# A third group's second layer as seven block products, with the weight sums moved earlier

## The chip, the cores and the metric

The kernel runs on one core of a Trainium2 chip. The metric is the device time of one execution in microseconds (us). The engines are TensorE (PE; PEld is its weight load), VectorE (DVE), ScalarE (ACT), GpSimd (POOL) and SyncE (SP, which issues most transfers here). Each engine works through its own queue in order and waits on semaphores for the others.

## The reference

Two stages follow each other. The first is a linear attention with decay over 4 batches, 8 heads, 768 positions and head size 64, in blocks of 64 positions; the second takes its output as x (4 x 768 rows of 512) through a layer norm and two dense layers.

```python
intra = einsum('bhic,bhjc->bhij', qb, kb) * Dmask          # lam ** (i - j), lower triangle
out   = einsum('bhij,bhjd->bhid', intra, vb) + einsum('bhid,bhde->bhie', qb * lam_pow, kv_state)
kv_state = lam ** block * kv_state + einsum('bhsd,bhse->bhde', kb * rev_pow, vb)
...
xn  = (x - mean) / sqrt(var + 1e-6) * g_ln
out = x + maximum(xn @ w_ch1, 0) @ w_ch2                   # w_ch1 512 x 2048, w_ch2 2048 x 512
```

## The kernel before

The 3072 rows are cut into 12 windows of 256 positions of one batch (`NU = 12`), called pairs below: a pair holds two tiles of 128 rows. Pair u belongs to batch u mod 4, so four pairs in a row are independent and pair u + 4 needs the state that pair u left. The attention's part of pair u yields x, its mean and `xc` = (x - mean) * g. The two dense layers work on groups; group g is pair g.

**The attention's part of a pair.** `in_k_one`, `in_q_one` and `in_v` cast and scale the loaded k, q, v (L231, L236, L242) on the engine that the call names. `transpose_kq(u, a, eng)` transposes k (a = 0) or q (a = 1) on TensorE into a PSUM bank of the tag `sc` (L260) and copies it to SBUF on `eng` (L261). `kv` makes the key-value products (L321), `scores` the block scores (L276) into two banks of the tag `mm` ("sce", early) or `sc`, `mask` multiplies them by the triangle on VectorE (L286), `new_state` sums and decays the state (L331 on VectorE, L327 on GpSimd), `av` and `inter` add up the output (L433, L446), `norm` takes x, its mean and `xc` (L472, L473 on ScalarE, L474 on VectorE), `rstd_of` takes the squares and the root on ScalarE (L514, L515) and the reciprocal on VectorE (L519), and `to_xT` transposes `xc` (L504) and copies it on ScalarE (L505). `s12` is kv, both scores and the masks of a pair; `Y(u)` interleaves kv and scores of pair u with the output of pair u - 1; `X(u)` does so for the later pairs, whose blocks are cut differently (`kv64`, L386; `scores64`, L367; `mask64`, L373).

**The dense layers.** Layer 1 of a group (`m1`) is eight units of eight 128x256 matmuls (L541), each with a relu on ScalarE into `hT` (L544). For some quarters of some groups `m1.tile` cuts the unit by tile instead: 16 matmuls of 128x128 (L652), relu L655. The dict `tiles` says which.

Layer 2 has two forms. The plain one (`m2`) makes for each of two tiles 16 matmuls of 128x512 (L681) in four parts; a part named in `M2_SPLIT` is made as eight matmuls of 128x256. A finished tile is scaled and added to x by one VectorE instruction (L705). The block form (`m2.w`) treats hidden rows in pairs and output columns in halves as 2x2 blocks and makes seven block products instead of eight, 56 matmuls of 128x256 (L576), in four PSUM banks a to d: P1 into a, P2 into b, P7 into c, P5 into d, and then P6, P4 and P3 added on top of a, c and d. Each product is evicted when it is done: P1 and P7 by ScalarE and an add on GpSimd (L600 and L601, L608 and L609), the others by VectorE (L589). The block form needs sums of blocks of `hT`, made per group by `h_sums` on VectorE (L559, L560, L561, in two halves, 0 to 4 and 4 to 8), and sums of blocks of W2, made once by `w_sums(c, n)` for each quarter c (L806 and L807 for n = 0, L809 and L810 for n = 1, 16 instructions in all). Groups from `WG` on use the block form. The tiles `hs13`, `hs2`, `hs4` have one buffer each.

**What sets the order.** The order is written out by hand: `plan` is the list of dense units (eight of layer 1 and eight of layer 2 per group), and `units(n)` takes the next n; the calls between stand where each engine's queue is to have them. PSUM has four banks of the tag `mm`, used in turn by layer 1, layer 2, kv and the early scores: who comes next must wait until the instruction that reads the bank four uses ago is done. Two banks carry the tag `sc`, in turn too.

Of the kernel before, what the change touches and what calls it, by code (L numbers as in the profile page):

```python
# [17 lines left out]
def kernel(  # L18
# [11 lines left out]
    nc = tc.nc  # L30
# [9 lines left out]
    KB = DF // 128  # L40
# [1 line left out]
    NWC = 4  # L42
    eps = 1e-6
    XS = 64.0
    WG = 3
    M2_SPLIT = [(t, i) for t in (3, 5) for i in range(4)] + [(1, 3), (2, 3)]
    assert D == 64 and S % W == 0 and DM == 512

    ctx.enter_context(tc.manual_schedule())
# [43 lines left out]
    def load_in(u, name, eng):  # L93
        got = qkv_in[u][name]
        fill(got, name, u, slice(0, H), eng)
        qkv_in[u][name] = got.rearrange("p h (j d) -> p h j d", j=2)
# [132 lines left out]
    def in_k_one(u, eng, j):  # L229
        src = qkv_in[u]["k"].rearrange("p (a e) j d -> p a e j d", e=2)  # L230
        (eng.copy if eng is nc.scalar else eng.tensor_copy)(part(0, st[u]["kq"], ALL)[:, :, :, j], src[:, :, :, j])  # L231

    def in_q_one(u, eng, j):
        src = qkv_in[u]["q"].rearrange("p (a e) j d -> p a e j d", e=2)
        lq = (lam_q[:, :, j] if u < LB else lam_p[:, 0, :]).rearrange("p (a e) -> p a e", e=2)
        eng.tensor_tensor(part(1, st[u]["kq"], ALL)[:, :, :, j], src[:, :, :, j],  # L236
                          lq[:, :, :, None].to_broadcast([128, NP, 2, D]), op=ALU.mult)

    def in_v(u, eng, hs=ALL):
        n = hs.stop - hs.start  # L240
        lv = lam_v[:, hs, :, None] if u < LB else lam_p[:, 1, hs, None, None]
        eng.tensor_tensor(st[u]["vb"][:, hs], qkv_in[u]["v"][:, hs], lv.to_broadcast([128, n, 2, D]), op=ALU.mult)  # L242
# [248 lines left out]
    def to_xT(u, ab):  # L491
        s = st[u]
        t = 2 * u + ab
        g = group_of[t]
        i = t - groups[g][0]
        if i == 0:
            xT_of[g] = gp.tile([128, KA, GT * 128], BF16, tag="xT", bufs=3, name="xT")
        dst = xT_of[g][:, :, i * 128:(i + 1) * 128]
        if u < 2:
            xt = mm_tile([128, KA, 128], BF16, "xt")  # L500
        else:
            xt = ps.tile([128, KA, 128], BF16, tag=f"po{ab}", name="xt")
        for kk in range(KA):
            nc.tensor.transpose(xt[:, kk, :], s["xc"][:, ab, kk * 128:(kk + 1) * 128], ident)  # L504
        nc.scalar.copy(dst, xt)  # L505

    def rstd_of(u):
        s = st[u]
        std = wk.tile([128, 2], F32, tag="std", name="std")
        if "sum" in s:  # L510
            ss = xp.tile([128, 2], F32, tag="ss", name="ss")
            for ab in range(2):
                sq = wk.tile([128, DM], BF16, tag="sq", bufs=1, name="sq")
                nc.scalar.activation(sq, s["x"][:, ab], ACT.Square, bias=s["nmean"][:, ab:ab + 1], accum_out=ss[:, ab:ab + 1])  # L514
            nc.scalar.activation(std, ss, ACT.Sqrt, bias=eps_t, scale=XS * XS / DM)  # L515
        else:
            nc.scalar.activation(std, s["mv"][:, :, 1], ACT.Sqrt, bias=eps_t, scale=XS * XS)
        rstd = xp.tile([128, 2], F32, tag="rstd", name="rstd")
        nc.vector.reciprocal(rstd, std)  # L519
        x_keep[u] = (s["x"], rstd)  # L520
# [5 lines left out]
    def mlp(g):  # L526
# [134 lines left out]
        def m2(i, part):  # L661
            t = groups[g][i]
            if t == 2 * NU - 1:
                w = DM // 2
                if part % 2 == 0:
                    acc[i] = mm_tile([128, w], F32, "pm2h")
                z = part // 2
                for kk in range(part % 2 * 8, part % 2 * 8 + 8):
                    nc.tensor.matmul(acc[i], lhsT=hT[:, kk, i * 128:(i + 1) * 128],
                                     rhs=w2[kk // W2K][:, kk % W2K, z * w:(z + 1) * w],  # L670
                                     start=(kk == 0), stop=(kk == KB - 1))
                if part % 2 == 1:
                    finish_half(t, acc.pop(i), z, w)
                return
            if part == 0:
                acc[i] = mm_tile([128, DM], F32, "pm2")
            n_z = 2 if (t, part) in M2_SPLIT else 1
            for kk in range(part * 4, part * 4 + 4):
                for z in range(n_z):
                    zs = slice(z * DM // n_z, (z + 1) * DM // n_z)  # L680
                    nc.tensor.matmul(acc[i][:, zs], lhsT=hT[:, kk, i * 128:(i + 1) * 128], rhs=w2[kk // W2K][:, kk % W2K, zs],  # L681
                                     start=(kk == 0 and z == 0), stop=(kk == KB - 1), skip_group_check=t in (1, 2, 3, 5))
            if part == KB // 4 - 1:
                finish(t, acc.pop(i))

# [114 lines left out]
    def w_sums(c, n):  # L800
        v = w2[c].rearrange("p (k e) d -> p k e d", e=2)
        w = DM // 2
        b11, b12, b21, b22 = v[:, :, 0, 0:w], v[:, :, 0, w:], v[:, :, 1, 0:w], v[:, :, 1, w:]
        t1, t2, t3, t4 = (wt[c][:, :, i] for i in range(4))
        if n == 0:
            nc.vector.tensor_tensor(t1, b12, b11, op=ALU.subtract)  # L806
            nc.vector.tensor_tensor(t3, b12, b22, op=ALU.add)  # L807
        else:
            nc.vector.tensor_tensor(t2, b11, t3, op=ALU.subtract)  # L809
            nc.vector.tensor_tensor(t4, t2, b21, op=ALU.add)  # L810
# [86 lines left out]
    def s3(u):  # L897
        av(u, range(NP))
        inter(u, 0)
        if st[u]["S"][0][1] is None:  # L900
            norm(u, 0)
# [34 lines left out]
    def Y(u, sums=None):  # L936
        kv(u)
        av(u - 1, range(NP))
        inter(u - 1, 0, fence=False)
        reader(u - 1, act=True)  # L940
        scores(u, 0)
        scores(u, 1, early=True)
        inter(u - 1, 1)
        new_state(u, 0, nc.gpsimd)
        if sums is None:
            mask(u, 0, (0,))
        else:
            mask(u, 1, (0,))
        new_state(u, 1, nc.gpsimd)
        if sums is not None:  # L950
            mask(u, 1, (1,))
            m2s[sums].sums(4, 8)
        norm(u - 1, 0)
        norm(u - 1, 1)
        if sums is None:
            mask(u, 1)
            mask(u, 0, (1,))
# [91 lines left out]
    plan += [(m2b, 1, part) for part in range(KB // 4)]  # L1049
    for g in range(2, len(groups)):  # L1050
        m1, m2 = mlp(g)
        tiles = {2: (0, 1, 2), 5: (3,), 6: (2, 3), 7: (1, 2)}.get(g, ())
        for c in range(NWC):
            plan += [(m1.tile, c, i) for i in range(2)] if c in tiles else [(m1, 2 * c + i) for i in range(2)]
        if g >= WG:
            plan += [(m2.w, n) for n in range(8)]
        else:
            plan += [(m2, i, part) for i in range(len(groups[g])) for part in range(KB // 4)]
# [3 lines left out]
    def units(n):  # L1062
        for _ in range(n):
            f, *a = next(steps)
            f(*a)
# [18 lines left out]
    nc.scalar.activation(sqrt_first, eps_t, ACT.Sqrt)  # L1084
    rstd_of(0)
    rstd_of(1)
    units(2)
    open_window(3)
    in_k_one(3, nc.gpsimd, 0)
# [2 lines left out]
    in_v(3, nc.gpsimd)  # L1092
    units(2)
    s3(2)
    units(2)
    s4(2)
    in_k_one(3, nc.vector, 1)
    load_in(4, "v", nc.sync)
    units(2)
    to_xT(2, 0)  # L1100
    units(1)
    rstd_of(2)
# [10 lines left out]
    load_in(5, "v", nc.sync)  # L1113
    units(1)
    in_v(4, nc.gpsimd)
    units(3)
    w_sums(0, 0)
    transpose_kq(3, 0, nc.scalar)
    units(1)
    transpose_kq(3, 1, nc.scalar)  # L1120
    units(1)
    w_sums(0, 1)
    w_sums(1, 0)
    units(3)
    s12(3)
    units(5)
    w_sums(1, 1)
    open_in(6, False)
    load_in(6, "k", nc.sync)
    w_sums(2, 0)  # L1130
    w_sums(2, 1)
    w_sums(3, 0)
    units(1)
    transpose_kq(4, 0, nc.scalar)
    load_in(6, "q", nc.sync)
    units(1)
    transpose_kq(4, 1, nc.scalar)
    units(1)
    Y(4)
    open_window(5)  # L1140
    in_k_one(5, nc.gpsimd, 0)
    in_k_one(5, nc.gpsimd, 1)
    in_q_one(5, nc.gpsimd, 0)
    in_q_one(5, nc.gpsimd, 1)
    in_v(5, nc.gpsimd)
    load_in(6, "v", nc.sync)
    units(2)
    rstd_of(3)
    units(1)
    to_xT(3, 0)  # L1150
    to_xT(3, 1)
    open_in(7, False)
    units(1)
    w_sums(3, 1)
    open_window(6)
    transpose_kq(5, 0, nc.scalar)
    in_k_one(6, nc.gpsimd, 0)
    in_k_one(6, nc.gpsimd, 1)
    units(1)
    transpose_kq(5, 1, nc.vector)  # L1160
    units(1)
    in_q_one(6, nc.vector, 1)
    in_q_one(6, nc.vector, 0)
    store(0)
    units(2)
    m2s[3].sums(0, 4)
    units(4)
    load_in(7, "k", nc.sync)
    load_in(7, "q", nc.sync)
    load_in(7, "v", nc.sync)  # L1170
    open_window(7)
    Y(5, sums=3)
    open_in(8, False)
    units(4)
    in_v(6, nc.gpsimd)
    units(2)
# [14 lines left out]
    rstd_of(4)  # L1191
    in_k_one(7, nc.vector, 1)
    in_v(7, nc.gpsimd)
    units(2)
    X(6, rest=False)
    in_k_one(7, nc.scalar, 0)
    open_window(8)
    store(1)
    store(2)
    mask64(6, 1)  # L1200
    m2s[4].sums(0, 4)
    units(4)
    m2s[4].sums(4, 8)
# [192 lines left out]
```

## Time and profile before

| | |
|---|---|
| median of 3 runs | 219.79 us (218.43, 219.79, 221.13) |
| profiled execution | 220.35 us, span 218.6 us |
| TensorE clock granted | 1.00 |
| busy: PE, PEld, DVE, ACT, POOL | 206.5, 177.5, 141.8, 144.4, 86.2 us |
| W2 transfers landed (quarters 0 to 3) | 36.71, 39.34, 42.25, 45.30 us |
| group 2: layer 1, layer 2 on TensorE | from 55.30 to 63.3, from 63.33 to 73.4 us, with other work between |
| pair 3's scores, pair 4's Y | from 59.24, from 67.77 us |
| group 3's first layer-1 unit | from 73.84 us |

The profiled execution lasts 1.75 us longer than its span, which runs from the first to the last instruction. Times in the profile count from the span's start. A matmul's own duration in the trace contains the time in which it passes through; how many are made in a time is read from start to start. Idle time of an engine that is not the bound costs nothing by itself; what counts is what TensorE waits for.

### The profile page before, as it was taken

How to read it: one execution, taken by the hardware profiler on the slowest of the kernel's cores; microseconds unless marked ns; L12 is line 12 of the kernel's file. 1: busy time of each engine (PE TensorE's matmuls, PEld its weight loads, DVE VectorE, ACT ScalarE, POOL GpSimd, SP SyncE). 2: the span in 40 equal slices, each digit the busy share in tenths (PEclk: the TensorE clock that was granted, in tenths of full speed). 3: DMA queues.
4: the chain of work that ended last, by engine and by line, in shares of the span. 5: the costliest groups of instructions: out<-in, count | busy, mean ns of one | idle time of the engine just before them, and what ended most of it. 6: DMA issues, size and time to landing. Idle time of an engine off the chain costs nothing.

```text
span 218.6 us, 8079 instructions
## 1 busy us (share of the span) xinstructions
PE 206.5 (94%) x3525; PEld 177.5 (81%) x3525; DVE 141.8 (65%) x286; ACT 144.4 (66%) x315; POOL 86.2 (39%) x120
## 2 busy tenths in 40 slices
PE   1897999999999999999999989999999999999992
PEld 0586788559977988889889889999889889889881
DVE  2688351535896968868596764578775765866243
ACT  2788478444747765597876795876896875854630
POOL 5656058119712915922761280453291212002020
PEclk9999999999999999999999999999999999999999
DMA  3999999999999899958699021030030020220303
GB/s 107 300 244 182 164 270 192 202 305 269 298 204 224 200 215 260 232 111 165 127 237 241 13 48 51 3 99 3 3 96 3 20 79 3 57 45 3 96 0 96
DMA packets 64421, 29.88 MB, mean 137 GB/s; under 512 B 38529, under 2 KB 61569, under 8 KB 64386
## 3 DMA queue, kind: packets, MB, share of 16 engines
q1 hardware_dynamic: 59776, 24.97, 47.2%
q0 software_dynamic: 4224, 4.19, 12.2%
q8 instruction: 27, 0.44, 0.9%
q10 hardware_dynamic: 386, 0.20, 0.4%
q14 instruction: 8, 0.07, 0.1%
HBM read 27.27 MB, written 6.29 MB: 153 GB/s over the span
## 4 chain that ended last, share of the span: by engine, by line
PE 78%; ACT 7%; DMA 6%; DVE 5%; issue 1%; POOL 1%; POOLq 0%; DVEq 0%
PE pm L541 27%; PE pm L681 10%; PE pm1t L652 8%; PE pwa L576 6%; PE pwc L576 6%; PE pwd L576 5%; DMA w<-in_moe_w_ch_dram 4%; PE tp L260 3%; PE pwb L576 3%; DVE x L589 2%; DMA lam_b<-in_lam_dram 2%; PE xt L504 2%; ACT hT L544 1%; PE po L446 1%; ACT sq L514 1%; PE po L433 1%
## 5 line engine op out<-in xcount | busy, mean ns | idle before, releaser
L541 PE MATMUL pm<-xT,w 128*128 128x256 bf16 x608 | 70.9, 273 | 2.2 <-DMA w<-in_moe_w_ch_dram 1.5
L541 PEld LDWEIGHTS <-w 128*128 128x128 bf16 x608 | 58.2, 98 | 9.6 <-DMA w<-in_moe_w_ch_dram 1.7
L544 ACT ACTIVATE hT<-pm 128x512 f16<-128x512 f32 x76 | 44.3, 597 | 19.8 <-PE pm L541 19.6
L576 PEld LDWEIGHTS <-hs 128*128 128x128 f16 x288 | 27.2, 98 | 2.9
L601 POOL TENSOR_TENSOR x<-ev_u,x 128x256 f32<-128x256 f32 x9 | 6.6, 730 | 55.3 <-ACT ev_u L600 43.5
L327 POOL TENSOR_TENSOR Sn<-Stmp,lam_s 128x256 bf16<-128x256 f32 x16 | 9.9, 622 | 41.7 <-DVE Stmp L405 22.8
L559 DVE TENSOR_TENSOR hs<-hT 128x1024 f16<-128x1024 f16 x18 | 15.4, 856 | 15.0 <-ACT hT L544 12.7
L261 ACT COPY kqT<-tp 128x1024 bf16<-128x1024 bf16 x16 | 16.2, 1012 | 12.4 <-PE tp L260 12.4
L681 PE MATMUL pm<-w,hT 128*128 128x256 f16 (+1 forms) x136 | 22.7, 317 | 0.0
L576 PEld LDWEIGHTS <-hT 128*128 128x128 f16 x216 | 20.7, 98 | 2.3
L652 PE MATMUL pm1t<-xT,w 128*128 128x128 bf16 x320 | 19.3, 219 | 0.4 <-ACT xT L505 0.3
L652 PEld LDWEIGHTS <-w 128*128 128x128 bf16 x320 | 18.4, 98 | 1.0 <-issue 0.7
L681 PEld LDWEIGHTS <-hT 128*128 128x128 f16 x136 | 12.7, 98 | 6.0
L505 ACT COPY xT<-xt 128x512 bf16<-128x512 bf16 x24 | 14.0, 589 | 4.7 <-PE xt L504 4.2
L472 ACT ACTIVATE x<-po 128x512 f32<-128x512 f32 x18 | 10.6, 590 | 8.7 <-PE po L446 5.3
L655 ACT ACTIVATE hT<-pm1t 128x512 f16<-128x512 f32 x20 | 11.8, 597 | 5.6 <-PE pm1t L652 5.5
L474 DVE SCALAR_TENSOR_TENSOR xc<-po,nmean,g_row 128x512 bf16<-128x512 f32 x18 | 12.8, 743 | 2.1 <-ACT nmean L473 2.1
L514 ACT ACTIVATE sq<-x,nmean 128x512 bf16<-128x512 f32 x18 | 13.0, 721 | 0.3
L589 DVE SCALAR_TENSOR_TENSOR x<-pwd,rstd,x 128x256 f32<-128x256 f32 x18 | 8.6, 480 | 5.5 <-POOL x L609 5.3
L242 POOL TENSOR_TENSOR vb<-vin,lam_v 128x1024 bf16<-128x1024 f32 (+1 forms) x7 | 11.8, 1688 | 0.1
L242 POOL TENSOR_TENSOR vb<-vin,lam_p 128x1024 bf16<-128x1024 f32 x6 | 11.4, 1898 | 0.0
L589 DVE SCALAR_TENSOR_TENSOR x<-pwa,rstd,x 128x512 f32<-128x512 f32 (+1 forms) x18 | 10.3, 611 | 1.3 <-PE pwa L576 0.7
(141 smaller groups left out, 382.3 us busy)
## 6 DMA issues: line engine op xcount, KB each, us to landing
out_dram<-x SPq DMA_DIRECT2D x22, 256.0 KB, 3.8
w<-in_moe_w_ch_dram POOLq DMA_DIRECT2D x8, 512.0 KB, 8.5
kin<-in_k_dram SPq DMA_DIRECT2D x14, 256.0 KB, 5.0
qin<-in_q_dram SPq DMA_DIRECT2D x14, 256.0 KB, 5.4
vin<-in_v_dram SPq DMA_DIRECT2D x14, 256.0 KB, 5.2
kin<-in_k_dram SPq DMA_DIRECT2D x5, 512.0 KB, 6.7
qin<-in_q_dram SPq DMA_DIRECT2D x5, 512.0 KB, 6.9
vin<-in_v_dram SPq DMA_DIRECT2D x5, 512.0 KB, 7.3
```

Source lines behind the costliest of these rows:

```text
L242: eng.tensor_tensor(st[u]["vb"][:, hs], qkv_in[u]["v"][:, hs], lv.to_broadcast([128, n, 2, D]), op=ALU.mult)
L261: (eng.copy if eng is nc.scalar else eng.tensor_copy)(s["kqT"][:, a], tp)
L474: nc.vector.scalar_tensor_tensor(xc, in0=po, scalar=nm, in1=g_row, op0=ALU.add, op1=ALU.mult)
L505: nc.scalar.copy(dst, xt)
L514: nc.scalar.activation(sq, s["x"][:, ab], ACT.Square, bias=s["nmean"][:, ab:ab + 1], accum_out=ss[:, ab:ab + 1])
L541: nc.tensor.matmul(pm[:, b, :], lhsT=w1[n // W2K][:, kk, (n % W2K) * 128:(n % W2K + 1) * 128], rhs=xT_of[g][:, kk, 0:N], start=(b == 0 and ...
L544: nc.scalar.activation(hT[:, u * NB:(u + 1) * NB, 0:N], pm, ACT.Relu)
L559: nc.vector.tensor_tensor(s13, b[:, :, 1:2, :].to_broadcast([128, n, 2, 128]), b[:, :, 0:4:3, :], op=ALU.subtract)
L576: nc.tensor.matmul(pr[bank], lhsT=lhs(r), rhs=rhs, start=(first and r == 0), stop=(r == KB // 2 - 1), skip_group_check=True)
L589: nc.vector.scalar_tensor_tensor(out, in0=in0, scalar=r[ab], in1=in1, op0=ALU.mult, op1=ALU.add)
L652: nc.tensor.matmul(pm[:, b, :], lhsT=w1[c][:, kk, b * 128:(b + 1) * 128], rhs=xT_of[g][:, kk, i * 128:(i + 1) * 128], start=(b == 0 and kk ...
L681: nc.tensor.matmul(acc[i][:, zs], lhsT=hT[:, kk, i * 128:(i + 1) * 128], rhs=w2[kk // W2K][:, kk % W2K, zs], start=(kk == 0 and z == 0), s ...
```

## The change

`WG` goes from 3 to 2: group 2 (the third) uses the block form, so its layer 2 is 56 matmuls of 128x256 instead of 16 of 128x512 and 32 of 128x256. Its three uses of `m1.tile` become two, and the one of group 5 goes. `M2_SPLIT` names other parts of the first two groups' layer 2. All `w_sums` calls move forward, to lie between `rstd_of(1)` and `s12(3)`. `Y(4)` gets group 2's second half of `h_sums`, its masks of the first head pair move behind `to_xT(3, ...)`, and it stands behind all of group 2's layer 1 instead of inside its layer 2; the q copy of pair 4 moves to VectorE. Pair 5's q and v products on GpSimd stand behind group 2's first products. `Y(5)` stands one layer-1 unit earlier, and the second half of group 3's `h_sums` follows that unit instead of standing inside `Y`. `X(6)` stands one unit earlier.

```diff
-    WG = 3
-    M2_SPLIT = [(t, i) for t in (3, 5) for i in range(4)] + [(1, 3), (2, 3)]
+    WG = 2
+    M2_SPLIT = [(3, i) for i in range(4)] + [(t, i) for t in (0, 1, 2) for i in (2, 3)] + [(t, 1) for t in (1, 2)]
...
         if sums is not None:
             mask(u, 1, (1,))
-            m2s[sums].sums(4, 8)
+            if sums < 3:
+                m2s[sums].sums(4, 8)
...
-        tiles = {2: (0, 1, 2), 5: (3,), 6: (2, 3), 7: (1, 2)}.get(g, ())
+        tiles = {2: (0, 1), 6: (2, 3), 7: (1, 2)}.get(g, ())
...
     rstd_of(1)
+    w_sums(0, 0)
     units(2)
...
     s3(2)
+    w_sums(0, 1)
     units(2)
     s4(2)
     in_k_one(3, nc.vector, 1)
+    w_sums(1, 0)
     load_in(4, "v", nc.sync)
     units(2)
+    w_sums(1, 1)
     to_xT(2, 0)
...
     in_v(4, nc.gpsimd)
+    w_sums(2, 0)
     units(3)
-    w_sums(0, 0)
+    w_sums(2, 1)
     transpose_kq(3, 0, nc.scalar)
     units(1)
     transpose_kq(3, 1, nc.scalar)
     units(1)
-    w_sums(0, 1)
-    w_sums(1, 0)
+    w_sums(3, 0)
+    w_sums(3, 1)
     units(3)
     s12(3)
-    units(5)
-    w_sums(1, 1)
+    units(3)
+    m2s[2].sums(0, 4)
     open_in(6, False)
     load_in(6, "k", nc.sync)
-    w_sums(2, 0)
-    w_sums(2, 1)
-    w_sums(3, 0)
-    units(1)
     transpose_kq(4, 0, nc.scalar)
+    transpose_kq(4, 1, nc.vector)
+    units(1)
     load_in(6, "q", nc.sync)
-    units(1)
-    transpose_kq(4, 1, nc.scalar)
-    units(1)
-    Y(4)
+    Y(4, sums=2)
     open_window(5)
     in_k_one(5, nc.gpsimd, 0)
     in_k_one(5, nc.gpsimd, 1)
+    units(4)
     in_q_one(5, nc.gpsimd, 0)
     in_q_one(5, nc.gpsimd, 1)
     in_v(5, nc.gpsimd)
     load_in(6, "v", nc.sync)
-    units(2)
     rstd_of(3)
-    units(1)
+    units(2)
     to_xT(3, 0)
+    mask(4, 0, (0,))
+    units(1)
     to_xT(3, 1)
+    mask(4, 0, (1,))
     open_in(7, False)
     units(1)
-    w_sums(3, 1)
     open_window(6)
+    units(1)
     transpose_kq(5, 0, nc.scalar)
...
     transpose_kq(5, 1, nc.vector)
-    units(1)
     in_q_one(6, nc.vector, 1)
     in_q_one(6, nc.vector, 0)
...
     m2s[3].sums(0, 4)
-    units(4)
+    units(3)
...
     Y(5, sums=3)
     open_in(8, False)
+    units(1)
+    m2s[3].sums(4, 8)
     units(4)
...
     in_v(7, nc.gpsimd)
-    units(2)
+    units(1)
     X(6, rest=False)
...
     mask64(6, 1)
+    units(1)
     m2s[4].sums(0, 4)
```

## The prediction

> **What bounds the kernel.** I read the page's busy shares first, then busy time by stretch around the edits, then the chain that ended last, then the engines' timelines from 40 to 106 us.
>
> ```profile
> PE 206.5 (94%) x3525; PEld 177.5 (81%) x3525; DVE 141.8 (65%) x286; ACT 144.4 (66%) x315; POOL 86.2 (39%) x120
> ```
>
> TensorE is the bound; VectorE has a third of the span free, but that is an average. By stretch (length, then PE, PEld, DVE, ACT and POOL busy with counts, granted clock, DMA share, GB/s):
>
> ```profile
> 40.00:56.00 16.00, 16.00 (x201) 10.86 (x200) 8.30 (x19) 6.79 (x19) 8.08 (x9) 1.00 1.10 269
> 56.00:76.00 20.00, 20.00 (x415) 16.97 (x413) 17.65 (x30) 13.24 (x27) 9.66 (x11) 1.00 1.01 228
> 76.00:92.00 16.00, 16.00 (x296) 14.11 (x295) 13.24 (x25) 9.08 (x21) 8.71 (x10) 1.00 1.00 235
> 92.00:100.00 8.00, 7.91 (x221) 7.02 (x220) 5.22 (x12) 7.47 (x21) 3.03 (x5) 1.00 0.49 103
> ```
>
> TensorE never stops from 40 to 92 us, at full clock. Each saved PE microsecond counts, and so does each new PE wait. VectorE is 88% busy (17.65 of 20) where group 2 works. The chain names the one place nearby where another engine sets the pace, X(6):
>
> ```profile
> 94.70 0.29 ACT std L515
> 95.00 0.97 ACT hT L544 x2
> 96.08 0.38 PE po L446 x16
> ```
>
> TensorE's second `inter` of pair 5 waits there for ScalarE's queue, 0.09 us (8.00 less 7.91). Last, VectorE's timeline (start, length):
>
> ```profile
> 55.72 1.13 DVE L809 TENSOR_TENSOR wt<-w,wt 128x512 f16<-128x512 f16 x1
> 56.88 2.01 DVE L810 TENSOR_TENSOR wt<-wt,w 128x512 f16<-128x512 f16 x1
> ...
> 62.74 0.41 DVE L809 TENSOR_TENSOR wt<-w,wt 128x512 f16<-128x512 f16 x1
> ```
>
> The same W2 sum takes 0.41 us when GpSimd idles and 2.01 beside GpSimd's `vb` (56.52 to 58.61): it ends 0.28 after `vb` does. Instructions with a PSUM input, as L705, keep their 0.75 us there. So a sum waits out the GpSimd instruction in progress, and the next GpSimd instruction waits for the sum.
>
> **TensorE's work.** Group 2's layer 2 now is one plain tile and one split tile. Four 512-wide matmuls run from 48.08 to 48.94 (0.215 each), eight 256-wide from 53.98 to 54.85 (0.109): 16 x 0.215 + 32 x 0.109 = 6.93 us. Seven products are 56 x 0.109 = 6.10. Two layer-1 quarters (group 2's third, group 5's last) leave 128-wide halves (64 in 3.57 us, so 1.79 per quarter) for 256-wide ones (16 x 0.109 = 1.75): -0.04 each. Six more layer-2 parts of groups 0 and 1 are split, each 8 x 0.109 - 4 x 0.215 = +0.01. Together **-0.85 us**.
>
> **Added on the others.** VectorE gets six half-sums of group 2 (row means 0.86, 0.43, 0.45, twice: 3.5 us) and six evictions of 0.47 to 0.75 (3.1 us) for two L705 (1.5). ScalarE gets two evictions of 0.48, GpSimd two adds of 0.74. The sixteen W2 sums only move. The built order of instructions shows 56 L576 matmuls in place of group 2's 48 L681, so the change does what it says. SP's transfers keep their order; pair 5's k landed at 57.8 and is first used at 70.8, so no transfer turns late.
>
> **W2 sums ahead of the masks.** Chunk 0's four fit VectorE's idle times at 42.0 to 44.1 and 45.7 to 47.2, where it waits for TensorE and ScalarE: free, and 0.4 us late for each sum if that cover were gone, since the `xc` behind them feeds transposes at 47.85 and 48.94. Their data landed (by 45.3 for the last chunk). Chunks 1, 2 and 3 stand from 48.2 on ahead of pair 3's masks, with four L705 between, and beside an unbroken GpSimd row: two q products (1.01 each start to start), `vb` (1.87), two casts (0.58), two q, `vb`: 8.9 us. I alternate the queues as the rows do. Chunk 1 ends at 51.5 (L705 of 49.14 then goes 2.2 us late, but its PSUM bank is wanted only at 55.3), chunk 2 at 56.7, the fourth L705 at 57.4 (bank wanted at 57.98: 0.6 to spare), chunk 3 at 60.9. Pair 3's first mask starts at **60.8 instead of 59.68**. TensorE has three units (2.6 us) behind the scores, until 62.4, and then transposes pair 4's k into the bank of the third mask, now done at 63.0; the fourth is done at 63.6. Waits 0.58 + 0.15 = **+0.7**. Ends: 0 if the masks start by 60.3, 2.0 if sums and GpSimd run wholly one after the other (masks at 62.1).
>
> [...]
>
> **Pair 4's q copy.** `transpose_kq(4, 1)` goes from ScalarE to VectorE, behind mask, state sum (0.4) and group 2's first three half-sums (1.5, about 0.5 more if the state decay on GpSimd comes between). It ends at 66.5; Y(4), begun at 64.9, reaches the scores 0.9 later, at 65.8. **+0.5** (ends 0.25 and 0.7). In the products, pwb's bank waits for the second state sum: +0.1 (ends 0 and 0.1).
>
> **P3 of group 2.** rstd_of(3) now stands on ScalarE behind `ev_p`, and its reciprocal on VectorE ahead of P5's eviction, whose bank P3 continues. From P7's end: `ev_p` 0.6, two squares and the root 2.0 (93.00 to 95.00 in X(6)), reciprocal and eviction 0.5: 3.1. TensorE needs 3 x 0.87 + 0.22 = 2.8: 0.3 late; with POOL's adds behind two casts, and the second `xc` ahead of pwb's eviction, 0.6. I take **+0.45**, and 0.1 for the xT copy behind the squares (ends 0 and 0.6 together).
>
> **Group 3.** The last layer-1 unit moves behind Y(5). Its relu then stands behind norm's ScalarE work, which ended 3.76 us after Y's start (85.13 less 81.37); relu till 4.36, TensorE asks at 4.32; the second half-sum ends near 5.2, asked at 5.0. **+0.2** (ends 0 and 0.5). Pair 5's q and v products on GpSimd wait behind group 2's adds, till 74.7 and 76.6; TensorE asks for q at 76.9, for v at 81.7: nothing, but one for one if GpSimd ran over 2.2 us later.
>
> **X(6) a unit earlier.** The chain above is ScalarE's: one relu less (0.49) ahead of the fence, against 0.87 of TensorE's: 0.09 + 0.87 - 0.49 = 0.47 instead of 0.09, **+0.4** (ends 0 and 0.45).
>
> **Sum.** -0.85 + 0.7 + 0.5 + 0.1 + 0.55 + 0.2 + 0.4 = +1.6. The profiled execution took 220.35 (span 218.6 and 1.75 around it): 221.95. It lies 0.56 over the median of the three runs, 219.79, which gives 221.4; I say **221.7**. All low ends: 0.25 of waits, -0.6; all high: 2.0 + 0.7 + 0.1 + 0.6 + 0.5 + 0.45 = 4.35, +3.5.
>
> **Rivals.** *The saving arrives (0.27).* If GpSimd's row leaves gaps, the masks start by 60.3, the later waits overlap (a TensorE held at the scores gives the P3 chain time), and the net is -0.85 to +0.2: 219.5 from the profiled run, 218.9 from the median. For it: TensorE has no wait in 40 to 92 today, VectorE idles 7.7 us in 40 to 56, and the W2 sums that filled 74.3 to 76.9 are gone. Against: GpSimd's row from 48.8 to 58.6 is unbroken, and P3's wait follows from queue order alone.
>
> *VectorE becomes the bound (0.08).* VectorE's own work from 48.2 until pair 4's last mask near 76 is about 22 of 28 us (sums 5.0, L705 2.8, eight masks 4.9, state work and the q copy 2.0, half-sums 3.1, `xc` 1.4, evictions 2.7, small ones 0.5); the 18 instructions with two SBUF inputs each may wait for a GpSimd instruction. Past 60.3, each microsecond of mask delay is one of TensorE's. It decides if the first mask starts after 64: then 3.7 of transposes' wait and the other 1.75, less 0.85, +4.6: 225.0 or 224.4, slower than before by over 2%.
>
> *The other moves gain something that I miss (0.05).* TensorE idles 0.6 us in 125 to 130 and 0.26 in 105 to 125; if the new order closed all, and no wait came: 220.35 - 0.85 - 0.9 = 218.6.
>
> **Numbers.** Forecast 0.60, its own range 220.4 to 223.3. Over 80% with the saving and the high ends: 218.7 to 223.9. A difference of 2% (4.4 us) is about what a measurement of this kernel can tell from no change. Faster by that: 0.02, the product form is worth 0.4%. Slower: the VectorE case, 0.08. Within: 0.90.
>
> **What will show it.** Pair 3's first L286 mask at 60 to 61.5; an idle time of TensorE before the L260 transposes near 63, ended by VectorE; one before Y(4)'s L276, ended by L261 on VectorE; one before the last pwd of group 2, ended by L589 behind a reciprocal; 0.3 to 0.5 us before L446 in X(6), ended by ScalarE; busy TensorE down by 0.85. I am wrong if TensorE stays unbroken through 60 to 76, or if a transfer or a bank that I called spare ends a wait.

## The result, and the profile after

The changed kernel took **221.92 us** (median of 10 runs, 220.5 to 224.78), the kernel before 219.28 us beside it (10 runs, 218.43 to 221.13). The ratio is **1.0105** (95% interval 1.0068 to 1.0142): 1.5 to 3.1 us slower, which is less than the 2% named above and more than nothing. The profiled execution took 221.99 us, span 220.3. The ratios leave out executions over 1.5% longer than the fastest of their kernel, and three of the profiles below are of such executions: with no part split, with `rstd_of(3)` put back, and "the same, most moves put back".

The page of the changed kernel begins with the busy shares, and further down it has the shares of the chain that ended last, by engine:

```profile
PE 207.1 (94%) x3525; PEld 179.7 (82%) x3525; DVE 148.0 (67%) x297; ACT 144.3 (66%) x316; POOL 89.4 (41%) x122
...
PE 63%; DVE 17%; ACT 7%; DMA 6%; issue 2%; POOL 1%; SPq 1%; POOLq 0%; DVEq 0%
```

In the kernel before the row of the chain was:

```profile
PE 78%; ACT 7%; DMA 6%; DVE 5%; issue 1%; POOL 1%; POOLq 0%; DVEq 0%
```

VectorE has 6.2 us more work (141.8 before), and its share of the chain is 17% instead of 5%, TensorE's 63% instead of 78%. Busy time by stretch, same columns as before:

```profile
40.00:56.00 16.00, 16.00 (x243) 13.90 (x241) 13.42 (x26) 7.22 (x17) 9.57 (x9) 1.00 1.10 273
56.00:76.00 20.00, 18.14 (x373) 15.59 (x371) 18.03 (x33) 11.61 (x26) 11.85 (x13) 1.00 1.01 224
76.00:92.00 16.00, 15.85 (x293) 13.87 (x291) 12.48 (x24) 8.70 (x20) 6.97 (x9) 1.00 1.10 236
92.00:100.00 8.00, 7.53 (x222) 6.69 (x221) 4.72 (x12) 7.21 (x20) 4.18 (x6) 1.00 0.39 83
```

VectorE's busy time in the first stretch rose from 8.30 to 13.42 us: the W2 sums stand there now. TensorE, unbroken before from 40 to 92, idles 1.86 us in the second stretch and 0.47 in the fourth. Its timeline (start, length, then what ended the idle time ahead) names the places:

```profile
61.71 1.20 PE L260 MATMUL tp<-ident,kq 128*128 128x128 bf16 x16 [0.45 <-DVE mA L286]
...
65.05 0.35 PE L276 MATMUL sc<-kqT 64*64 64x128 bf16 x10 [0.18 <-DVE kqT L261]
66.43 0.30 PE L276 MATMUL sc<-kqT 64*64 64x128 bf16 x6 [1.03 <-issue]
...
72.97 0.27 PE L576 MATMUL pwd<-w,hs 128*128 128x256 f16 x1 [0.21 <-DVE x L589]
...
96.71 0.38 PE L446 MATMUL po<-Sn,kqT 64*64 64x64 bf16 x16 [0.47 <-ACT seen L457]
```

Four of the five were forecast, with what ends them: pair 3's mask, pair 4's q copy on VectorE, the eviction behind the reciprocal, X(6). The fifth, 1.03 us in the middle of pair 4's scores, was not: "issue" means that the profile shows nothing that TensorE waits for.

**How the parts are measured below.** A matmul's distance to the next, start to start, was nearly the same for each shape: 0.1094 us for 256 columns (its own record lasts 0.273, and so overlaps the next ones), 0.0562 for 128, 0.2152 for 512, and on average 0.0155 and 0.0086 for the two small shapes (64 rows; 128 and 64 columns). What a distance has over that, if more than 0.06, I call a wait; single waits next to the small shapes are good to 0.03, since their distances vary. All is counted over one *stretch*, from group 2's first layer-1 matmul to the span's end, since what lies ahead of it moves from execution to execution: that matmul started at 55.30 in the profile before and at 53.97 after, where a W1 quarter happened to land 1.4 us earlier (20.73 instead of 22.11). Work is the sum of the fixed distances.

| kernel | stretch | work | waits |
|---|---|---|---|
| before | 163.35 | 154.59 | 4.34 |
| changed | 166.31 | 153.68 | 8.14 |
| changed, profiled again | 165.38 | 153.68 | 7.25 |

So TensorE's work falls by 0.91 us, and the waits add 3.80 (or 2.91) to it. All kernels below compute the whole result.

### The profile page after: what moved, and what is told of

Same layout as the page of the kernel before. It is cut to its first block, busy times and chain, and to the rows that moved or that the text cites. A ratio compares the mean times of both kernels' runs of the same rounds, so it can differ in the third digit from the quotient of the medians.

```text
span 220.3 us, 8097 instructions
## 1 busy us (share of the span) xinstructions
PE 207.1 (94%) x3525; PEld 179.7 (82%) x3525; DVE 148.0 (67%) x297; ACT 144.3 (66%) x316; POOL 89.4 (41%) x122
## 4 chain that ended last, share of the span: by engine, by line
PE 63%; DVE 17%; ACT 7%; DMA 6%; issue 2%; POOL 1%; SPq 1%; POOLq 0%; DVEq 0%
PE pm L541 26%; PE pwd L576 6%; PE pwc L576 5%; PE pwa L576 5%; PE pm1t L652 4%; DMA w<-in_moe_w_ch_dram 3%; DVE x L589 3%; PE pm L681 3%; PE pwb L576 3%; DMA qin<-in_q_dram 3%; PE tp L260 2%; DVE xc L474 2%; DVE mA L286 2%; PE xt L504 2%; DVE wt L807 1%
## 5 line engine op out<-in xcount | busy, mean ns | idle before, releaser
L541 PE MATMUL pm<-xT,w 128*128 128x256 bf16 x640 | 74.9, 273 | 1.3 <-DVE x L589 0.6
L541 PEld LDWEIGHTS <-w 128*128 128x128 bf16 x640 | 61.1, 98 | 9.3 <-issue 0.8
L544 ACT ACTIVATE hT<-pm 128x512 f16<-128x512 f32 x80 | 46.8, 597 | 21.9 <-PE pm L541 21.7
L576 PEld LDWEIGHTS <-hs 128*128 128x128 f16 x320 | 30.2, 98 | 3.8 <-DVE hs L559 0.6
L559 DVE TENSOR_TENSOR hs<-hT 128x1024 f16<-128x1024 f16 x20 | 16.8, 839 | 15.5 <-ACT hT L544 13.6
L261 ACT COPY kqT<-tp 128x1024 bf16<-128x1024 bf16 x15 | 15.2, 1012 | 10.6 <-PE tp L260 10.6
L652 PE MATMUL pm1t<-xT,w 128*128 128x128 bf16 x256 | 15.4, 219 | 0.9 <-DMA w<-in_moe_w_ch_dram 0.5
L681 PE MATMUL pm<-w,hT 128*128 128x256 f16 (+1 forms) x112 | 14.9, 288 | 0.0
L589 DVE SCALAR_TENSOR_TENSOR x<-pwa,rstd,x 128x512 f32<-128x512 f32 (+1 forms) x20 | 11.4, 612 | 1.4 <-PE pwa L576 0.7
L589 DVE SCALAR_TENSOR_TENSOR x<-pwb,rstd,x 128x256 f32<-128x256 f32 x10 | 4.8, 482 | 11.0 <-POOL x L601 11.0
L655 ACT ACTIVATE hT<-pm1t 128x512 f16<-128x512 f32 x16 | 9.4, 597 | 4.2 <-PE pm1t L652 4.2
L576 PE MATMUL pwa<-w,hT 128*128 128x256 f16 x80 | 12.0, 273 | 0.0
```

The lines of the kernel that those rows point to most:

```text
L261: (eng.copy if eng is nc.scalar else eng.tensor_copy)(s["kqT"][:, a], tp)
L541: nc.tensor.matmul(pm[:, b, :], lhsT=w1[n // W2K][:, kk, (n % W2K) * 128:(n % W2K + 1) * 128], rhs=xT_of[g][:, kk, 0:N], start=(b == 0 and ...
L544: nc.scalar.activation(hT[:, u * NB:(u + 1) * NB, 0:N], pm, ACT.Relu)
L559: nc.vector.tensor_tensor(s13, b[:, :, 1:2, :].to_broadcast([128, n, 2, 128]), b[:, :, 0:4:3, :], op=ALU.subtract)
L576: nc.tensor.matmul(pr[bank], lhsT=lhs(r), rhs=rhs, start=(first and r == 0), stop=(r == KB // 2 - 1), skip_group_check=True)
L589: nc.vector.scalar_tensor_tensor(out, in0=in0, scalar=r[ab], in1=in1, op0=ALU.mult, op1=ALU.add)
```

## The experiments

All ratios are to the kernel before, run beside each. The profile with no part split is not comparable: in 3.41 us of its stretch, from 90.62, TensorE's granted clock was 0.50. In that with `rstd_of(3)` put back the clock was 0.50 from 21.35 to 28.18, ahead of the stretch.

| kernel | median (before beside it) | ratio, 95% interval | stretch | waits |
|---|---|---|---|---|
| changed, again | 222.0 (219.4) | 1.0124, 1.0093 to 1.0155 | 165.38 | 7.25 |
| all parts split | 221.38 (219.4) | 1.0134, 1.0061 to 1.0207 | 164.78 | 6.76 |
| no part split | 225.94 (219.4) | 1.0282, 1.0223 to 1.0341 | - | - |
| last W2 sums behind pair 4's q copy | 222.65 (219.4) | 1.0132, 1.007 to 1.0195 | 165.18 | 7.07 |
| all split, X(6) put back | 221.16 (219.08) | 1.0077, 1.0045 to 1.0108 | 165.06 | 7.00 |
| all split, rstd_of(3) put back | 221.16 (219.08) | 1.0096, 1.006 to 1.0132 | 164.43 | 6.33 |
| all split, most moves put back | 221.02 (219.08) | 1.0108, 1.0061 to 1.0154 | 164.75 | 6.69 |
| **before**, no part split | 222.71 (219.08) | 1.018, 1.0128 to 1.0232 | 165.57 | 6.59 |
| all split, sums earlier | 219.87 (218.87) | 1.0024, 0.9998 to 1.0051 | 163.91 | 5.80 |
| the same, most moves put back | 219.14 (218.87) | 1.0003, 0.9976 to 1.003 | 164.72 | 6.71 |
| the same, last sums behind L705 | 219.59 (219.05) | 1.0025, 0.9999 to 1.0052 | 163.53 | 5.42 |
| changed, split list of before for groups 0, 1 | 222.27 (218.87) | 1.0129, 1.0091 to 1.0168 | 165.50 | 7.40 |

### The hole in pair 4's scores

First: does it come back, and does it hang on the number of instructions? A layer-2 part is made as 8 matmuls instead of 4 when it is split, which is 4 matmuls and 4 weight loads more and hardly any time (8 x 0.1094 less 4 x 0.2152, 0.014 us). One kernel splits all 16 parts of tiles 0 to 3 (the second line of the diff), one splits none (the third).

> The changed kernel once more. In its first profile TensorE stood still for 1.03 us in the middle of pair 4's scores (L276), 10 matmuls in, with no semaphore to wait for. Theory I (instruction supply): TensorE's instructions arrive by 16 KB transfers, and the one that it needs there comes late, since a whole transfer's worth of small attention matmuls is used up in 1.5 us; the stream is the same, so the hole recurs at the same matmul, 0.8 to 1.3 us. Rival (chance): no hole there, and the time between group 2's first L652 and the end is 1.0 us shorter than the 166.3 us of the first profile. Time by both 221 to 222.5.

```diff
-    M2_SPLIT = [(3, i) for i in range(4)] + [(t, i) for t in (0, 1, 2) for i in (2, 3)] + [(t, 1) for t in (1, 2)]
+    M2_SPLIT = [(t, i) for t in range(4) for i in range(4)]
+    M2_SPLIT = []
```

> All 16 parts of the first two groups' layer 2 split instead of 12: 32 more TensorE instructions ahead of Y(4), 0.04 us more work, no other queue touched. Theory I: every boundary of the 16 KB transfers falls 32 instructions earlier in the work, before the dense stretch, so the transfer is asked for about a unit (0.9 us) earlier: the hole in the scores falls from 1.0 to under 0.3 us, and the time by 0.8. Rival (a data or bank wait that the profile does not name): the hole stays at the same matmul, 1.0 us, and the time is up by 0.04.

> No part split: 96 fewer TensorE instructions ahead of Y(4) than in the changed kernel, 0.12 us less work. Theory I: the boundary falls 96 instructions later in the work; a hole, if any, is no longer at the 10th score matmul but some 48 matmuls later (in the early scores or the first products), 0 to 0.8 us. Rival (data or bank wait): the hole stays at the 10th score matmul, 1.0 us; time down by 0.12.

The hole came back at the same matmul, 0.76 us long (0.8 to 1.3 expected). With all parts split TensorE's timeline shows the scores in one piece:

```profile
65.68 0.42 PE L276 MATMUL sc<-kqT 64*64 64x128 bf16 x16 [0.18 <-DVE kqT L261]
65.90 0.42 PE L276 MATMUL sce<-kqT 64*64 64x128 bf16 x16
```

The stretch is 0.6 us shorter than in the repetition (0.8 expected); the ratio, 1.0134, does not show it, but its interval is 1.5% wide. With no part split, holes stand in five places, the first of them in the products (and the kernel is 2.8% slower than before, the largest effect of any edit here; the lowered clock has a part in its profile):

```profile
71.25 0.38 PE L576 MATMUL pwc<-wt,hs 128*128 128x256 f16 x2
73.38 0.83 PE L576 MATMUL pwc<-wt,hs 128*128 128x256 f16 x6 [1.75 <-issue]
```

Is it the new order? The kernel *before* with no part split answers that:

```diff
-    M2_SPLIT = [(t, i) for t in (3, 5) for i in range(4)] + [(1, 3), (2, 3)]
+    M2_SPLIT = []
```

> The kernel before, with no layer-2 part split: 80 fewer TensorE instructions, 0.1 us less work, nothing else touched. Theory I (instruction supply depends on where the 16 KB boundaries fall): holes without a semaphore to wait for appear in TensorE's dense attention stretches behind group 1's layer 2, 1 to 5 us in all, and the kernel is slower by that. Rival (the split parts only cost their 0.1 us, and the holes belong to the changed order): no hole, time down by 0.1.

```profile
82.31 0.34 PE L276 MATMUL sce<-kqT 64*64 64x128 bf16 x10
84.56 0.30 PE L276 MATMUL sce<-kqT 64*64 64x128 bf16 x6 [1.91 <-issue]
```

That one hole, 2.13 us from matmul to matmul, makes nearly all of its 2.22 longer stretch. (The median is 3.6 us longer; the last section says what the record shows of the rest.) So such a hole does not need the change. This one stands in scores again, but with no part split the first stood in the products. The sharpest test undoes only the change's new list for the first two groups: 6 parts fewer are split, so 24 matmuls (48 TensorE instructions) fewer run ahead of the place.

```diff
-    M2_SPLIT = [(3, i) for i in range(4)] + [(t, i) for t in (0, 1, 2) for i in (2, 3)] + [(t, 1) for t in (1, 2)]
+    M2_SPLIT = [(3, i) for i in range(4)] + [(1, 3), (2, 3)]
```

> The changed kernel with the list of split layer-2 parts undone for groups 0 and 1: six parts fewer are split, 48 TensorE instructions fewer before group 2. Theory 'instruction supply': the boundaries of the 16 KB transfers fall 48 instructions later in the work, so the 0.8 to 1.0 us hole in pair 4's scores moves by about 24 matmuls to behind the scores, or changes size, and shows as idle time without a semaphore within some 3 us of the old place; time 221 to 222.5. Rival 'the hole belongs to the scores' (their operands or bank): it stays at the same matmul of L276 with 0.75 or more. Rival 'the split itself costs or gains': the time follows the instruction count, 48 fewer matmul pairs' worth, under 0.1 us.

```profile
65.76 0.42 PE L276 MATMUL sc<-kqT 64*64 64x128 bf16 x16 [0.18 <-DVE kqT L261]
65.98 0.42 PE L276 MATMUL sce<-kqT 64*64 64x128 bf16 x16
66.20 0.22 PE L446 MATMUL po<-Sn,kqT 64*64 64x64 bf16 x2
67.27 0.28 PE L446 MATMUL po<-Sn,kqT 64*64 64x64 bf16 x6 [0.84 <-issue]
```

The hole was behind the 10th matmul of the first scores; now it is behind 6 + 16 + 2 = **24 matmuls** later, exactly the 24 that are missing. The rival of the operands falls, since the hole left the scores. The rival by which the time follows the count foresaw under 0.1 us, which the time cannot tell: the ratio 1.0129 lies beside 1.0105 and 1.0124 of the changed kernel. With no part split (48 fewer) the first hole is 6 + 16 + 8 + 7 + 7 + 1 + 1 + 2 = 48 matmuls later.

### The W2 sums

Is the wait for pair 3's masks the price, and can it be moved away? First by moving the last quarter's sums behind pair 4's q copy (only this, with the change's own split list):

```diff
     units(1)
-    w_sums(3, 0)
-    w_sums(3, 1)
     units(3)
     s12(3)
...
     transpose_kq(4, 1, nc.vector)
+    w_sums(3, 0)
+    w_sums(3, 1)
     units(1)
```

> The four W2 sums of the last quarter moved from ahead of pair 3's masks to behind pair 4's q copy on VectorE. Theory Q (each wait is a place in VectorE's queue): pair 3's first mask starts as soon as its scores are there, 1 us earlier against group 2's first L652; the waits of 0.6 and 0.15 us before pair 4's transposes (L260) and the 0.25 before the scores' first matmul go: time down by 1.0, to 220.9, if the hole in the scores keeps its 1.0. Rival (VectorE has no room at all in this stretch): the 1.6 us of sums reappear as a wait before pwa or pwb, whose banks wait for the state sums behind them, and the time stays at 221.9.

```profile
66.58 0.93 PE L576 MATMUL pwa<-w,hT 128*128 128x256 f16 x7 [1.12 <-DVE Stmp L331]
```

The waits at L260 and L261 went, and so did the hole: counted from group 2's start, the transfer of instructions that it hangs on (last section) began 2.2 us earlier (7.8 instead of 10.0); why is not shown. But 1.28 us now stands ahead of the first product, for the state sum behind the moved W2 sums. The rival held: the time, 222.65, did not fall.

Then the other way: six of the eight pairs of sums one place earlier, into the time in which VectorE idled in 42 to 46 us and GpSimd had not yet begun its row (all parts split; nothing else differs from that kernel). The pairs of chunk 2 and the first of chunk 3 move likewise; the last pair stays alone ahead of `s12(3)`.

```diff
     rstd_of(1)
     w_sums(0, 0)
+    w_sums(0, 1)
...
     s3(2)
-    w_sums(0, 1)
+    w_sums(1, 0)
...
     in_k_one(3, nc.vector, 1)
-    w_sums(1, 0)
+    w_sums(1, 1)
...
```

> The changed kernel with all parts of layer 2 split and with each pair of W2 sums one place earlier, nothing else. Theory: pair 3's first mask starts about 1 us earlier than with the same split and the sums where the change put them (stretch 164.78), so the waits at the L260 transposes (0.51 + 0.15) go and that at pair 4's scores (0.34) shrinks to 0.1: stretch 163.9 to 164.2, time 220.4 to 220.9. Rival 'a wait that goes comes back at the next bank': 0.6 or more returns before the products of group 2, stretch 164.6 to 165, time 221.2 to 221.8.

VectorE's timeline, the last sum and the first mask, first in the kernel before and in the changed kernel:

```profile
59.15 0.41 DVE L807 TENSOR_TENSOR wt<-w 128x512 f16<-128x512 f16 x1
59.68 1.29 DVE L286 TENSOR_TENSOR mA<-sce,keep 128x512 bf16<-128x512 f32 x2
```

```profile
59.10 0.42 DVE L810 TENSOR_TENSOR wt<-wt,w 128x512 f16<-128x512 f16 x1
59.45 1.28 DVE L286 TENSOR_TENSOR mA<-sce,keep 128x512 bf16<-128x512 f32 x2
```

Then in this kernel, with TensorE's at the two places:

```profile
57.15 2.01 DVE L810 TENSOR_TENSOR wt<-wt,w 128x512 f16<-128x512 f16 x1
59.31 1.29 DVE L286 TENSOR_TENSOR mA<-sce,keep 128x512 bf16<-128x512 f32 x2
```

```profile
62.05 1.06 PE L260 MATMUL tp<-ident,kq 128*128 128x128 bf16 x16
...
64.92 0.42 PE L276 MATMUL sc<-kqT 64*64 64x128 bf16 x16
```

Both waits are gone, the stretch is 163.91 (expected 163.9 to 164.2), the median half a microsecond under what was expected (as is that of the kernel before beside it, 218.87 against 219.4), and the ratio falls from 1.0134 to 1.0024, with intervals that just do not meet. **This one edit takes back most of the loss:** 0.87 of the 1.43 us by which the stretch with all parts split exceeds that of the kernel before. Counted from group 2's start, the mask begins at 4.38 us, as in the kernel before, instead of 5.47 in the changed kernel and 5.38 with all parts split. The sum beside `vb` still takes 2.01 us; what helped is that two sums fewer stand behind each point of GpSimd's row.

### The other moves

X(6) a unit later again, all parts split:

```diff
     in_v(7, nc.gpsimd)
-    units(1)
+    units(2)
     X(6, rest=False)
...
     mask64(6, 1)
-    units(1)
     m2s[4].sums(0, 4)
```

> All 16 parts split, and X(6) back behind four of group 4's layer-1 units. Theory Q (each wait is a place in a queue): the 0.63 us before the second inter of pair 5, ended by ScalarE, falls to the 0.24 of the kernel before; the stretch from group 2's first L652 to the end goes from 164.8 us (all parts split) to 164.4. Rival: ScalarE's relu of the unit put back comes ahead of the fence again and the wait stays above 0.5; nothing gained.

X(6)'s wait fell from 0.63 to 0.24, its size before the change, but the stretch grew by 0.28: a hole of the kind above opened a little behind it.

```profile
96.45 0.38 PE L446 MATMUL po<-Sn,kqT 64*64 64x64 bf16 x16
96.76 2.14 PE L541 MATMUL pm<-xT,w 128*128 128x256 bf16 x18
99.60 1.59 PE L541 MATMUL pm<-xT,w 128*128 128x256 bf16 x13 [0.70 <-issue]
```

`rstd_of(3)` back behind pair 5's q copy, all parts split:

```diff
-    rstd_of(3)
     units(2)
     to_xT(3, 0)
...
     transpose_kq(5, 1, nc.vector)
+    rstd_of(3)
```

> All 16 parts split, and rstd_of(3) (two squares, the root, the reciprocal) moved behind pair 5's q transpose, as it stood before. Theory Q: the 0.37 us before P3's first matmul, ended by L589 behind the reciprocal, falls under 0.15, and the stretch from group 2's first L652 to the end goes from 164.8 to 164.5. Rival (P5's eviction is late because of GpSimd's adds and the second xc, not because of the reciprocal): the wait stays at 0.3 or more.

P3's wait fell only from 0.37 to 0.30, so the rival held. The stretch came to 164.43, near the theory's 164.5, but by other waits: those at the masks and at pair 4's scores, 1.02 together, are gone from it, and one of 0.47 for a L705 stands at layer 1. Group 2 began 3 us later in this execution: TensorE had waited 2.23 us for W1 and then had a clock of 0.50 for 6.83. The reciprocal was a small part of P3's wait; the second `xc` and GpSimd's adds, which I had priced beside it, are what is left by elimination, not by a run of their own.

These two together, and pair 4's q copy on ScalarE, Y(5) back ahead of group 3's last unit, and the last two W2 sums behind group 2's second half-sums:

```diff
-    transpose_kq(4, 1, nc.vector)
+    transpose_kq(4, 1, nc.scalar)
...
             m2s[sums].sums(4, 8)
+            if sums == 2:
+                w_sums(3, 1)
...
```

> The seven products of group 2 kept; all 16 parts split; X(6), Y(5) and rstd_of(3) back where they stood before the change; pair 4's q copy on ScalarE; the last two W2 sums behind pair 4's early masks and group 2's second half-sums. Theory Q with I: no hole in TensorE's stream, the waits in groups 2 and 3 and in X(6) go except for some 0.3 us; the products' 0.85 us stand: the stretch from group 2's first L652 to the end is 162.5 to 163.0 us against 163.35 of the kernel before, time 0.3 to 0.8 under it. Rival (VectorE is full from 48 to 77 us, so that a wait taken away comes back at the next bank): the stretch stays over 164, time 1 us over the kernel before.

Group 3's wait (0.14) and X(6)'s (0.24) were as before the change, L260 and L261 did not wait; but three waits of 0.38, 1.09 and 0.55 us stand in and between group 2's products, and the rival held:

```profile
69.84 0.38 PE L576 MATMUL pwa<-wt,hs 128*128 128x256 f16 x2 [0.22 <-DVE wt L809]
70.05 0.38 PE L576 MATMUL pwc<-wt,hT 128*128 128x256 f16 x2
71.37 0.40 PE L504 MATMUL xt<-ident,xc 128*128 128x128 bf16 x4 [0.93 <-DVE xc L474]
...
72.80 0.27 PE L576 MATMUL pwd<-w,hs 128*128 128x256 f16 x1 [0.39 <-DVE x L589]
```

VectorE worked without a gap from 65.2 to 75.9 us, and idled in only two places, 0.98 us together, from 47.4 on. What was put later there was late for its reader or for the next bank. So the same moves were joined to the earlier sums:

> Keeps the seven products and all parts of layer 2 split; X(6), Y(5) and rstd_of(3) at their places of before the change, pair 4's q copy on ScalarE, and the W2 sums moved the other way: each pair of sums one place earlier, so that (0,0), (0,1), (1,0) and (1,1) stand in VectorE's idle time of 42 to 46 us, ahead of GpSimd's unbroken row, and the last two stand ahead of pair 3's masks. Stretch from group 2's first layer-1 matmul to the span's end: 163.35 before the change, 164.75 with the last two sums behind Y(4). Theory 'the price is VectorE's time in 48 to 76 us': two sums less there and about 1.6 us less waiting beside GpSimd, so the waits of 0.38, 1.09 and 0.55 in group 2 shrink together to under 0.8: stretch 162.8 to 163.6, time 218.7 to 219.6 beside a before of 219.1. Rival 'VectorE is as full as it was, only in another order': the first mask moves by under 0.5, waits of 1.5 or more stay in group 2, stretch 164.4 or more, time 220.5 to 221.3. An 'issue' hole of TensorE over 0.5 in group 2 would cloud both and is to be taken off before reading.

In its profile the three waits shrank to P3's 0.30, and a new one of 1.66 us appeared ahead of them, at layer 1 (first TensorE's, then VectorE's timeline):

```profile
59.53 1.05 PE L652 MATMUL pm1t<-xT,w 128*128 128x128 bf16 x16 [1.50 <-DVE x L705]
```

```profile
50.76 2.12 DVE L807 TENSOR_TENSOR wt<-w 128x512 f16<-128x512 f16 x1
...
56.36 2.12 DVE L806 TENSOR_TENSOR wt<-w 128x512 f16<-128x512 f16 x1
58.40 0.41 DVE L807 TENSOR_TENSOR wt<-w 128x512 f16<-128x512 f16 x1
58.74 0.74 DVE L705 SCALAR_TENSOR_TENSOR x<-pm,rstd,x 128x512 f32<-128x512 f32 x1
```

Two sums met GpSimd's two `vb`, and the fourth L705 stood behind the second. The profiled execution took 221.62 us, the median 219.14: the stretch says "rival" and the ratio, 1.0003, says "theory", and how often the 1.66 stands in the other executions is not shown. The ratio is what counts for the time. The last run puts that L705 ahead of the sums:

```diff
     in_v(4, nc.gpsimd)
     w_sums(2, 1)
     units(3)
-    w_sums(3, 0)
     transpose_kq(3, 0, nc.scalar)
     units(1)
     transpose_kq(3, 1, nc.scalar)
     units(1)
+    w_sums(3, 0)
     w_sums(3, 1)
```

> The kernel with the W2 sums one place earlier and the other moves taken back (stretch 164.72, of which 1.66 is one wait of TensorE for the fourth L705, which stood behind two sums caught by GpSimd's vb), with the last quarter's first two sums now behind that L705 instead of ahead of it; nothing else differs. Theory 'the saving of 0.85 arrives when no VectorE work that frees a bank stands behind the sums': the 1.66 goes, waits in group 2 together under 0.6, stretch 162.6 to 163.3 against 163.35 before the change, time 0.1 to 0.7 below the kernel before. Rival 'VectorE is too full in any order': the masks come late in its place, a wait of 0.5 or more stands at the transposes or at Y(4)'s products, stretch 163.8 or more, time 0.3 or more above the kernel before.

The 1.66 went, and group 2's waits were 0.41 together, as the theory had it. But a 0.43 hole stands before L541 at 97.70, ended by "issue", at the place where the kernel with X(6) put back had its hole; the stretch came to 163.53, and the time to 1.0025 of before instead of under it. Without the hole the stretch would be 163.1, 0.25 under before. The median lies 0.54 above the one beside it, and 0.18 of that are in the stretch; where the rest lies is not shown. **No version here beat the kernel before;** the best ones equal it.

## Why the prediction was right, and where it was not

The forecast was 221.7 us, or +1.6 on the profiled execution; measured were 221.92, and +2.3 by the ratio (1.5 to 3.1). Direction and rough size came out, and the time is closer than the terms deserve. Counted over the stretch of the two profiles they stand so:

| term, as the prediction put it | forecast | measured |
|---|---|---|
| TensorE's work | -0.85 | -0.91 |
| W2 sums ahead of the masks (L260) | +0.7 | +0.76 (0.61 + 0.15) |
| pair 4's q copy (L276 behind L261) | +0.5 | +0.34 |
| second state sum at the products (pwb) | +0.1 | none; 0.11 at pwc, behind group 2's second half-sums (L559) |
| P3 behind the reciprocal, and xT copy | +0.55 | +0.31 (0.37, less the 0.13 that this wait has in group 3 before; xT copy 0.07) |
| group 3's second half-sums | +0.2 | +0.31 |
| X(6) a unit earlier | +0.4 | +0.38 |
| **instruction supply** | **none** | **+1.21** (0.94 in the second execution) |
| Smid (L402), at 113.51 | none | +0.17 |
| rest, each about 0.1 or less | none | +0.28 |
| sum | +1.6 | +2.96 |

- **TensorE's work and the built order** held: the +0.06 of the six split parts lies ahead of the stretch, and the rest of the term is -0.91.
- **W2 sums ahead of the masks.** The walk through the queues said that the first mask starts at 60.8. It started at 59.45, 1.35 earlier than walked, in an execution whose group 2 began 1.33 earlier: the size was right to 0.02. The alternation of sums and GpSimd's instructions is what the rows show: 1.15 us for the L810 at 48.49, 2.12 for the L807 beside `vb`, 0.42 for a sum alone. GpSimd's instructions took longer beside the sums too (two q products 2.40 us from 48.16 on and 2.06 from 71.98 on, `vb` 2.08 at 56.25 and 1.91 at 73.99), and group 2's half-sum L561 took 0.71 beside GpSimd's cast at 70.03 and 0.42 at 63.97 with GpSimd idle, while L705 kept 0.74. The forecast's high end, sums and GpSimd's row wholly one after the other and masks at 62.1, is 1.3 us too late beside 60.8 in the same count. The forecast had no wait for masks up to 60.3, which is 5.0 us behind group 2's start. In the profiles in which TensorE is not held up ahead of the transposes, masks at 5.47, 5.38, 5.26, 5.09 and 4.93 us cost 0.76, 0.66, 0.55, 0.38 and 0.22, and masks up to 4.56 cost nothing: one for one, from about 4.7 on. The changed kernel has 0.76 in one profile and 0.22 in the other, so the wait varies between executions of one order. That its cause is the sums' place is shown by the kernel with the sums earlier.
- **Free cover.** I let the first four sums lie in idle time at 42 to 47 and the twelve others behind. The room there was larger than the change used: in the kernel with the sums earlier six stand ahead of 46 us, without any wait for it.
- **Pair 4's q copy** was sized 0.16 too high. The copy ended at 64.99, where the walk, moved by 1.33, has 65.17. That the wait at the masks had already given VectorE part of that time, an overlap of the kind that the first rival named, is argued and not shown.
- **P3** was the term most oversized. Putting `rstd_of(3)` back takes 0.07 off, so the reciprocal ahead of the eviction was not the main part.
- **The step that failed** is the way TensorE was priced, by its matmuls and its semaphores alone ("Six more layer-2 parts of groups 0 and 1 are split, each 8 x 0.109 - 4 x 0.215 = +0.01"): nothing said that its instructions themselves must arrive, and the sum has no term for it. It cost 1.21 us, more than any term that was forecast. The split list is not the cause of the hole either, as its undoing moved the hole by 24 matmuls and left it 0.84 long. What decided in these runs is where a fixed count of instructions falls in the order (every 128 matmuls with their weight loads), and how late their transfer came: at the eleven stops of the last section TensorE went on 1.2 to 1.5 us after the landing.
- **Rivals.** "The saving arrives" failed for the changed kernel, but its condition (masks by 60.3, counted 5.0 us from group 2's start) is what the earlier sums met; then the ratio was 1.0024, no loss that can be told from noise, but no saving either. "VectorE becomes the bound" did not go to its 4.6 us; its milder form, no room left in 48 to 76, is what the kernels with the last sums moved back showed.
- **The closeness of 221.7** has luck in it: in the profiled execution 1.33 us of earlier start hide the 1.21 of the hole, and the forecast was set 0.3 above the median's own sum. By the ratio the loss is 2.3 us, 0.7 more than the +1.6 of the terms.

## What to carry to other kernels

Read the idle time of an engine as a place with two ends: for the W2 sums VectorE's third of free time was worth something ahead of 48 us and little behind it. Moving twelve of the sixteen sums one place earlier took 0.87 us off the stretch, while moving some of them later only renamed the wait. When TensorE stops with no semaphore in a run of small matmuls, count its matmuls from the start. Here the number stayed while the matmuls ahead of it changed (1119 in three kernels, 1375 in two of different order), which pointed to the instruction supply, and few instructions ahead of it moved the stop: 48 fewer moved it by 24 matmuls, and with 32 more TensorE passed the place without one. Price a change by where each wait comes back, not by the wait that it removes.

## What the runs showed of the hardware

**TensorE's instructions came in pieces of 256, and at eleven of 364 seams between them it stood still.** The page's row for the queue whose transfers keep step with its matmuls (packets, MB, share):

```profile
q8 instruction: 27, 0.44, 0.8%
```

That is 27 transfers of 16,384 bytes over about 7,050 TensorE instructions (3525 matmuls, a weight load each), some 261 per transfer; the stops give the count more closely. In all seven profiles (of six kernels) in which TensorE stopped for over 0.2 us with no semaphore behind 50 us (eleven stops), 128k + 95 matmuls, with k a whole number, stand ahead of the stop: 1119 in the changed kernel, in its repetition, with the old split list and with no part split; 1375 in the kernel before with no part split; 1375, 1631, 2527 and 2783 with no part split; 1759 in two of the four kernels with X(6) put back. 128 matmuls are 256 instructions (64 bytes each, by division of a transfer), so I take these places for the seams between two transfers. By their order I count the k-th transfer to the k-th seam. At the eleven stops TensorE goes on 1.2 to 1.5 us after the last transfer has landed and 2.2 to 3.1 after it began (in the changed kernel: begun 63.95, landed 64.92, on at 66.43). The fourteen profiles have 353 more such seams, passed without a stop; TensorE passed 340 of them over 1.52 us after the landing, and none earlier than 0.98 after it or 2.36 after the beginning; in the kernel before the closest pass is 1.61 and 2.57 (at 17.52), behind 50 us 2.72 and 4.04. The 128 matmuls ahead of the seam in the changed kernel took 4.0 us, in the kernel before 3.6 without a stop; there the transfer had begun 0.8 us ahead of the previous seam, in the changed kernel 1.5 behind it. Why it is asked for earlier or later stays open. A crowd of other transfers is not needed: two of the stops with no part split, at 156 and 170, fall where the DMA share is 0.35 and 0.12. The fastest piece, nearly all of attention's small matmuls, was used up in 1.49 us (kernel before with no part split, ahead of 68.76), less than the 2.2 us and more that lay between a transfer's beginning and TensorE's going on at every seam, so it matters there first.

So 353 of the 364 seams cost no stop. At the other eleven TensorE was idle for 0.2 to 2.5 us, and taking 40 matmuls out of the first three groups made the kernel before 1.8% slower (1.28 to 2.32), with one such hole in its profile.

**A stop of 2.48 us was followed by a halved clock.** Behind the hole of 2.48 us in the profile with no part split the granted clock fell to 0.50 for 3.41 us (from 90.62). The only others of that kind in the fourteen profiles, between the first 18 us and TensorE's last matmuls, stand at the waits of 2.15 and 2.23 us for W1, for 3.41 and 6.83 us; with idle times of up to 1.91 there was none. One such piece costs about 1.7 us by an estimate (half of 3.41). This would fit the kernel before with no part split: its profiled execution, with a hole of 1.91, took 222.07 us at a mean granted clock of 1.00, and two of the other three took 223.34 and 223.93 at 0.992. That the hole was over 2 us in those two is not shown.
